# Batch 0's queries and keys loaded as whole rows of nine tokens, in a kernel of attention and two expert layers

## The chip, the cores and the metric

One core of a Trainium2 chip runs the whole program. The metric is the device time of one execution in microseconds, and less is better. The core has TensorE (PE) for products, VectorE (DVE), ScalarE (ACT) and GpSimd (POOL) for work on elements, and SyncE (SP), whose queue issues nearly all of this kernel's transfers.

## The reference

Three blocks follow each other. Attention has 4 batches, 8 heads, 576 tokens of 64 numbers, all float32. It is the sum of two parts: a pooled one, in which queries, keys and values are means over groups of four tokens, and a local one, in which a token sees only tokens less than four away. The result, 2304 rows of 512, goes through a layer with ELU (512 to 2048 to 512) and a gated layer with SiLU (512 to 1536 to 512). The weights are given in double precision.

```python
q_d = q.reshape(B, H, Sd, 4, D).mean(axis=3)           # k_d, v_d alike
out_up = np.repeat(sm_attn(q_d, k_d, v_d), 4, axis=2)  # softmax attention, scaled
scores = np.where(np.abs(pos[:, None] - pos[None, :]) < 4, scale * q @ k.T, -1e9)
x = out_up + softmax(scores) @ v                       # as rows of (batch, token)
h = x @ w_in
x = np.where(h > 0, h, np.exp(np.minimum(h, 0)) - 1) @ w_out
return (silu(x @ w_gate) * (x @ w_val)) @ w_o2
```

## The kernel before

The order in which each engine works is fixed when the program is built. A planner (class `Work`) holds a list of tasks; `add` gives each one its engine or engines, an assumed cost, a due time and the tasks and buffers that it needs. `run` plays them through on assumed clocks and lets each engine take the ready task with the earliest key; the instructions are written in the order so found, and every engine runs its own in that order, waiting on semaphores. `urge` replaces the due times of everything that the first product of the first layer needs by the length of the chain that still follows. The constants in capitals (`SECOND`, `START`, `STEP`, `LATE`, ...) are due times, offsets and penalties of the planner. They change no computation, only the order.

The first layer takes 288 rows of x (a chunk, three units of 96 tokens) at a time through 16 steps, one for each 128 columns of `w_in`: a product with a piece of `w_in` (L1010 to L1012, three products each, with both sides split in a high and a low part), the ELU on ScalarE and VectorE, and a product with `w_out`. Chunk 0's second product (L1044) uses plain float32. Each piece of weights comes as 512 KB in double precision and is made into words by ScalarE (L515, L509) and VectorE (L513, L519, through a PSUM bank) and split by a cast (L352, L356) and a subtraction on GpSimd (L554).

Chunk 0 can begin when its three units of batch 0 are through attention, so what stands ahead of it is a start-up, and there the change lies:

- `load_ident`, `load_mask`, `warm_up` and `clear` (L1692 to L1720): the identity, the masks, seven products that feed TensorE nothing of use, and a clear of the transposed queries `qT` and keys `kT`, whose margins must be zero.
- `add_first_batch` (L719): for each pair of heads p, half u of the tokens, and queries or keys, a load of 72 rows (L728; a row has four tokens of each of two heads, 1 KB a head), eight products with the identity that turn it (L734), a copy out of PSUM to `qT` or `kT` (L352 on ScalarE, L354 on VectorE), and a sum over each four tokens (`add_sums`: L620 on VectorE, or L625 and L626 on GpSimd).
- `add_pooled` (L785), for each pair of heads of batch 0: two loads of values (L800), sums of them on GpSimd (L795, L796), the score products (L812), maxima (L819, L820), exps (L825), norms (L831 to L835), transposes of the weights (L850) and the products with the values (L866).
- `add_local` (L630), for each unit: its values' loads (L595), score products (L640), mask, maximum, exps, sum, weights (L658 to L680), a spread into a block matrix (L352), products with the values (L709).
- `add_split` (L979): the two parts of attention are added (L987), and x is split for the first layer in a cast and a subtraction (L998).

The later batches come by other ways (`add_turned`, `add_pooled_all`), while the first layer's products run. The second layer follows at the end.

Of the kernel before, what the change touches and what calls it, by code (L numbers as in the profile page):

```python
# [9 lines left out]
F32 = mybir.dt.float32  # L10
# [9 lines left out]
P = 128  # L20
R = 4
# [5 lines left out]
U = NB * SB  # L27
CR = 64
NEG = -1e9
UPC = 3  # L30
# [106 lines left out]
class Work:  # L137
# [4 lines left out]
    LATENCY = 0.15  # L142
    SECOND = 43.48
    CHANGE = 0.15
# [157 lines left out]
def attention_moe_moe(ctx: ExitStack, tc: tile.TileContext, q, k, v, w_in, w_out, w_gate, w_val, w_o2, ident_in, mask_in, band_in, picks_in, out):  # L302
    nc = tc.nc
    B, H, S, D = q.shape
    FF1 = w_out.shape[0]
    FF2 = w_o2.shape[0]
    G = S // R
# [67 lines left out]
    def att_bank(late=False):  # L375
        return banks.new(lambda: [4, 5] if late or begun else [6, 0, 1, 2, 3, 7])
# [5 lines left out]

    STEP2 = 7.68
    START = 42.2
    STEP0 = 4.8
    STEP = 4.66
    FIRST = -40.0
    VALUES = -84.37
    LATER = 168.39
    POOLED = -4.59  # L390
    EARLY = -2.13
    PREFER = -27.09
    EAGER = 40.21
    URGENT = 26.74
    FREE = 7.77
    SLACK = 0.0
    LOAD = 14.4
    KEEP0 = 4.31
    KEEP1 = 1.69
    DIRECT = 2, 3, 1  # L400
    PARTS1 = 57.15
    UNIT1 = 2.61
    LAGG = 2
    MASK = -16.54
    TAILW = True
    WOS0 = 30.76
    WOS1 = 0.93
    EARLYA = 22.91
    EARLYB = 12.5
    LOADA = 53.93  # L410
    LOADB = -5.71
    O2A = 62.58
    O2B = 29.71
    ELU1 = 19.39
    ELU0 = 19.41
    UNIT2 = 22.59
    UNIT0 = 10.8
    RAW = 31.93
    DEPTH = 6
    PARTS = 13.09  # L420
    OUT = -5.4
    SUMS = 8.14
    SUMS3 = 11.07
    SECOND2 = 14.25
    LATE = 82.24
    AWAY0 = 1.99
    AWAY1 = 6.63
    LO1 = 15.73
    HI1 = 11.94
    LO2 = 26.21  # L430
    HI2 = 28.33
    LO3 = 26.82
    HI3 = 0.91
    KEYS = 34.63
    POOL1 = -7.86
    POOL0 = 10.55
    POOL2 = 13.16
    LOCAL = 0.63
    ROWS = 24.96
    INPUT = -2.86  # L440
    order = [(c, f) for c in range(NC) for f in range(NF1)]
# [106 lines left out]
    def add_weight_split(key, due, w, copiers=COPIER, second=0):  # L548
# [25 lines left out]

    PAD, LONG = R - 1, S + 8
    turned = {
        name: pools["att"].tile(shape, F32, tag=name, name=name)
# [141 lines left out]
    def add_first_batch(rows, ready):  # L719

        sums[0] = sum_ring.new()
        parts = {name: [longs[name].new(lambda p=p: [p]) for p in range(NP)] for name in ("qT", "kT")}
        made = {}
        for k, (p, u, which) in enumerate((p, u, which) for p in range(NP) for u in range(2) for which in range(2)):
            name, start = (("qT", 0), ("kT", PAD))[which]
            t, dst, pt = rows[k], parts[name][p], att_bank()
            cols = slice(start + u * UPC * U, start + (u + 1) * UPC * U)
            add("sp", 0.5, FIRST + 0.5 * k, lambda t=t, p=p, u=u, name=name: nc.sync.dma_start(  # L728
                out=t.t, in_=rows_of(name[0], 0, u, 2 * p, 2 * p + 2)), writes=[t], nbytes=HALF * 2048 * 1.2)

            def turn(t=t, pt=pt):
                for r in range(R):
                    for j in range(2):
                        nc.tensor.matmul(  # L734
                            pt.t[j * D:(j + 1) * D, :UPC * U].rearrange("c (g r) -> c g r", r=R)[:, :, r],
                            t.t[:, j, r * D:(r + 1) * D], ident[:HALF, :HALF], start=True, stop=True)

            add("pe", 0.56, FIRST + k - EAGER, turn, reads=[t], writes=[pt, dst], slack=SLACK, kind="small", after=ready[:1], words=32)
            made[which, p, u] = add(COPIER, (0.41, 0.45), FIRST + k + 1, lambda engine, dst=dst, pt=pt, cols=cols: copy(
                engine, dst.t[:, cols], pt.t[:, :UPC * U]), reads=[pt], writes=[dst], second=1)  # L740
            summed.setdefault((0, p), []).append(add_sums(
                FIRST + k + 2, lambda dst=dst, cols=cols: dst.t[:, cols].rearrange("p (g r) -> p g r", r=R),
                lambda which=which, p=p, u=u: sums[0].t[:, which, p, u * HALF:(u + 1) * HALF], [], [sums[0]], (0.45, 0.73),
                holds=[dst], after=[made[which, p, u]], engines=EITHER))
        return parts, made
# [38 lines left out]

    def add_pooled(b, p, due, load_due, raws, pr, prT):  # L785

# [11 lines left out]
        for u in range(2):  # L798
            t = raws[u]
            add("sp", 0.5, load_due, lambda u=u, t=t: nc.sync.dma_start(  # L800
                out=t.t, in_=rows_of("v", b, u, 2 * p, 2 * p + 2)), writes=[t], nbytes=HALF * 2048 * 1.2)
            rowed.append(add("pool", 1.18, due, lambda t=t: add_rows(t.t), reads=[t]))


# [58 lines left out]
        def values():  # L863
            for j in range(2):
                for w in range(2):
                    nc.tensor.matmul(  # L866
                        pv.t[j * D:(j + 1) * D, :G], raws[w].t[:, j, :D], prT.t[:, j, w], start=(w == 0), stop=(w == 1))

        valued.append(add("pe", 1.4, due + 6 - EAGER, values, words=16, reads=[prT], holds=raws, after=rowed, writes=[pv, xdT[b]], slack=SLACK, kind="small"))
        add(COPIER, (0.28, 0.3), due + 6.5 - FREE, lambda engine: copy(engine, xdT[b].t[:, p], pv.t[:, :G]), reads=[pv], writes=[xdT[b]], second=1)  # L870
# [789 lines left out]
    with tc.manual_schedule():  # L1660
# [8 lines left out]

        rows = [x for _ in range(2 * NP) for x in parts(2)]  # L1670
        vals = [x for _ in range(NU // 2) for x in parts(2)]
        praws = [x for _ in range(NP) for x in parts(2)]
# [3 lines left out]
        sms = [Part(x.whole, x.whole.t.rearrange("p a b -> p (a b)")[:, 4 * G:4 * G + H * QB].bitcast(F32).rearrange("p (n h k) -> p n h k", n=1, h=H))  # L1676
               for x in (*probs, rows[0], rows[4])]
        turneds = [Part(rows[4 * p].whole, probs[p].t) for p in range(NP)]
        for t in turneds:
            t.t = t.whole.t.rearrange("p a b -> p (a b)")[:HALF, :4 * G].bitcast(F32).rearrange("p (j u k) -> p j u k", j=2, u=2)  # L1680
        for t in rows + praws:
            t.t = t.t[:HALF].rearrange("p (h x) -> p h x", h=2)

# [19 lines left out]
        add("pe", 1.5 + 0.42 * WARM, -1000.0, warm_up)  # L1703
        add("pool", 4.8, -1000.0, clear)
        add("act", 2.0, -1000.0, table)
# [20 lines left out]
        for n in range(NU):  # L1726
            late = n >= UPC
            add("sp", 2.0, LATER + n if late else VALUES + n, lambda n=n: load_values(0, n * U, vals[n].t), writes=[vals[n]], nbytes=P * H * D * 4 * 3.1)
            turned_by = [t for (which, p, u), t in made.items() if u == (late or 0) or (which and (n == UPC - 1 or n == UPC))]
            if n == UPC:  # L1730
                for p in range(NP):
                    add_pooled(0, p, POOLED + 1.7 * p, -28 + p, raws=praws[2 * p:2 * p + 2], pr=probs[p], prT=turneds[p])
            xfs[n], = add_local(n, 1, 0.1 * n + LATE * late, parts, turned_by, [vals[n]], ready[1:], valued if late else (), sms[n])
# [92 lines left out]
```

## Time and profile before

| | |
|---|---|
| median of 3 runs | 938.55 us (938.22 to 938.77) |
| the profiled execution | 937.54 us, its span 935.8 us |
| TensorE busy | 913.0 us (98%) |
| VectorE, ScalarE, GpSimd busy | 566.3, 523.1, 533.6 us |
| mean granted TensorE clock | 0.978 of 2.4 GHz |

The span runs from the first to the last instruction of the profiled execution. The granted clock is what the throttle lets TensorE have: 1.00 is 2.4 GHz, 0.50 is 1.2 GHz. A float32 product appears in the records as two matmuls and two weight loads, a transpose as one. `SPq` is SP's queue, `PEld` TensorE's weight loads.

### The profile page before, as it was taken

Reading aid. Unit: us, or ns where it says so; the run is one execution under the profiler, and the core shown is the slowest. Engines: PE = TensorE matmul, PEld = TensorE weight load, DVE = VectorE, ACT = ScalarE, POOL = GpSimd, SP = SyncE. Lnnn points to the kernel's source line nnn. Section 1 sums busy time; section 2 is a strip of 40 time slices with the busy share of each in tenths; the row PEclk is TensorE's granted clock in tenths of the full one; section 3 lists DMA queues with packets and bytes.
Section 4 is the critical chain, followed back from the end, with each engine's and each line's share of the span. In section 5 each row is a group of like instructions: output and inputs, shape, how many; then the busy total and the mean of one; then the engine's idle time right before and its main releaser. Section 6 shows DMA issues by size and latency. Waiting matters only on the chain.

```text
span 935.8 us, 19972 instructions
## 1 busy us (share of the span) xinstructions
PE 913.0 (98%) x7573; PEld 829.0 (89%) x7573; DVE 566.3 (61%) x937; ACT 523.1 (56%) x1125; POOL 533.6 (57%) x609
## 2 busy tenths in 40 slices
PE   8779999999999999999999999999999999999998
PEld 7568889999999999999999888887888887999998
DVE  2988777777677249444337385435434247896773
ACT  3988566454556457675665456555546435453441
POOL 6797956664665459489791408998899940000000
PEclk7589999999999999999999999999999999999999
DMA  6999445659745654565588613452554299854331
GB/s 172 309 270 276 82 125 126 139 178 315 132 114 152 189 186 140 163 204 195 187 296 326 247 61 124 169 191 91 210 181 183 104 350 308 273 170 135 127 113 46
DMA packets 194704, 172.12 MB, mean 184 GB/s; under 512 B 96176, under 2 KB 166192, under 8 KB 194608
## 3 DMA queue, kind: packets, MB, share of 16 engines
q1 hardware_dynamic: 194464, 170.58, 58.2%
q8 instruction: 60, 0.98, 0.4%
q14 instruction: 36, 0.29, 0.1%
q10 hardware_dynamic: 144, 0.26, 0.1%
HBM read 111.62 MB, written 59.18 MB: 183 GB/s over the span
## 4 chain that ended last, share of the span: by engine, by line
PE 91%; DMA 4%; DVE 2%; SPq 1%; ACT 1%; issue 1%; POOL 0%; DVEq 0%
PE bank L1010 28%; PE bank L1011 27%; PE bank L1012 27%; PE bank L1044 3%; PE bank L640 2%; PE bank L709 2%; DMA w<-in_v_dram 2%; DMA w<-in_moe_w_in_dram 1%; DMA w<-in_k_dram 1%; PE bank L915 1%; PE bank L909 1%; PE bank L962 1%; DVE xh L1191 1%; SPq L595 0%; DMA wd<-mid 0%
## 5 line engine op out<-in xcount | busy, mean ns | idle before, releaser
L1010 PE MATMUL bank<-xs,wu 128*128 128x512 f32 x336 | 133.4, 397 | 2.4 <-DVE blk L1223 2.0
L1012 PE MATMUL bank<-xs,wu 128*128 128x512 f32 x336 | 133.2, 396 | 0.0
L1011 PE MATMUL bank<-xs,wu 128*128 128x512 f32 x336 | 133.2, 396 | 0.0
L1010 PE MATMUL bank<-os,ys 128*128 128x256 f32 x378 | 107.2, 283 | 1.0 <-DVE o L1223 1.0
L1011 PE MATMUL bank<-os,ys 128*128 128x256 f32 x378 | 107.0, 283 | 0.0
L1012 PE MATMUL bank<-os,ys 128*128 128x256 f32 x378 | 106.9, 283 | 0.0
L1010 PE MATMUL bank<-x,w 128*128 128x288 f32 x320 | 100.2, 313 | 1.4 <-DVE e L1088 0.9
L1010 PE MATMUL bank<-g,w 128*128 128x288 f32 (+1 forms) x320 | 101.0, 316 | 0.0
L1223 DVE TENSOR_TENSOR blk<-bank,blk 128x512 f32<-128x512 f32 x72 | 49.5, 690 | 81.7 <-PE bank L1012 75.4
L1011 PE MATMUL bank<-g,w 128*128 128x288 f32 (+1 forms) x320 | 98.5, 308 | 0.0
L1012 PE MATMUL bank<-g,w 128*128 128x288 f32 (+1 forms) x320 | 98.3, 307 | 0.0
L1011 PE MATMUL bank<-x,w 128*128 128x288 f32 x320 | 95.3, 298 | 0.0
L1012 PE MATMUL bank<-x,w 128*128 128x288 f32 x320 | 94.9, 296 | 0.0
L1095 POOL TENSOR_TENSOR g<-e,g 128x288 fp32r<-128x288 f32 x64 | 57.2, 894 | 56.0 <-ACT g L352 44.7
L1220 ACT COPY blk<-bank 128x512 f32<-128x512 f32 x72 | 42.0, 585 | 72.9 <-PE bank L1012 66.0
L1010 PEld LDWEIGHTS bank<-xs,wu 128*128 128x128 f32 x336 | 63.3, 188 | 17.7 <-DVE blk L1223 2.9
L1012 PEld LDWEIGHTS bank<-xs,wu 128*128 128x128 f32 x336 | 63.3, 188 | 15.4
L1011 PEld LDWEIGHTS bank<-xs,wu 128*128 128x128 f32 x336 | 63.3, 188 | 14.0
L1010 PEld LDWEIGHTS bank<-os,ys 128*128 128x128 f32 x378 | 72.5, 192 | 1.6 <-DVE o L1223 1.4
L1011 PEld LDWEIGHTS bank<-os,ys 128*128 128x128 f32 x378 | 72.5, 192 | 0.1
L1012 PEld LDWEIGHTS bank<-os,ys 128*128 128x128 f32 x378 | 72.5, 192 | 0.0
L1191 POOL TENSOR_TENSOR wu<-s,wu 128x256 fp32r<-128x256 f32 x79 | 59.7, 783 | 18.5 <-ACT wu L1194 18.4
(213 smaller groups left out, 2525.3 us busy)
## 6 DMA issues: line engine op xcount, KB each, us to landing
yr<-yd SPq DMA_DIRECT2D x27, 512.0 KB
yd<-blk SPq DMA_DIRECT2D x24, 512.0 KB
os<-od SPq DMA_DIRECT2D x42, 256.0 KB
w<-in_moe_w_in_dram SPq DMA_DIRECT2D x16, 512.0 KB
w<-in_moe_w_out_dram SPq DMA_DIRECT2D x16, 512.0 KB
wp<-w SPq DMA_DIRECT2D x16, 512.0 KB
wu<-wp SPq DMA_DIRECT2D x16, 512.0 KB
u<-wd SPq DMA_DIRECT2D x32, 256.0 KB
```

Of the source, the lines that this page charges most:

```text
L640: nc.tensor.matmul(sc[j].t[s * QB:(s + 1) * QB, (u * NP + p) * QB:(u * NP + p + 1) * QB], parts["qT"][p].t[j * D:(j + 1) * D, a:a + QB], p ...
L709: nc.tensor.matmul(pvs[u].t[j * D:(j + 1) * D, p * U:(p + 1) * U], tvs[u].t[:, (2 * p + j) * D:(2 * p + j + 1) * D], bd.t[:, u, j * NP + p ...
L909: nc.tensor.matmul(sc[0].t[j * D:(j + 1) * D, 2 * G:3 * G], vs0.t[:, w, j], prT0.t[:, j, w], start=(w == 0), stop=(w == 1))
L915: nc.tensor.matmul(sc[j].t[:HALF, u * G:(u + 1) * G], t[:, 0, p, u * HALF:(u + 1) * HALF], t[:, 1, p], start=True, stop=True)
L1010: nc.tensor.matmul(ps, sh, mh, start=first, stop=False, skip_group_check=more)
L1011: nc.tensor.matmul(ps, sh, ml, start=False, stop=False, skip_group_check=more)
L1012: nc.tensor.matmul(ps, sl, mh, start=False, stop=last, skip_group_check=more)
L1044: nc.tensor.matmul(acc[0][i].t[:, :T1], wo.t[:, i * P:(i + 1) * P].bitcast(F32), ge(), start=f == 0, stop=f == NF1 - 1)
L1095: add("pool", 0.86, due - URGENT, lambda e=e, g=g: nc.gpsimd.tensor_tensor(out=g.t[:, 1], in0=e.t, in1=g.t[:, 0], op=ALU.subtract), reads= ...
L1191: return task(engines, n, due, lambda engine=engines[0]: two(engine).tensor_tensor(out=out(), in0=in0(), in1=in1(), op=op), reads, writes, ...
L1220: return add("act", ps_copy, when(m) - 20, lambda: nc.scalar.copy(d(i), ps.t[:, :w]), reads=[ps], writes=of(i))
L1223: return add("dve", ps_sum, when(m) - 20, lambda: nc.vector.tensor_tensor(out=d(i), in0=ps.t[:, :w], in1=d(i), op=ALU.add), reads=[ps], wr ...
```

## The change

Batch 0's queries and keys are loaded as 128 rows (two heads times 64 groups of nine tokens), one load for each pair of heads. Each is turned by eighteen products of 64 rows, five tokens into one PSUM bank and four into another; two copies put them in place with a stride of nine. One sum over each pair of heads takes the place of two. Every local unit of batch 0 now waits for all copies. The pooled values come in one load for each pair, in rows of eight tokens, so that the pooled queries and keys are taken alternately instead of by halves. The clear touches only the margins of `qT` and `kT`. The planner's costs and its constants are set anew.

```diff
-    SECOND = 43.48
+    SECOND = 37.4
-    START = 42.2
-    STEP0 = 4.8
-    STEP = 4.66
+    START = 43.14
+    STEP0 = 4.77
+    STEP = 4.73
...
-    VALUES = -84.37
-    LATER = 168.39
+    VALUES = -89.48
+    LATER = 136.26
...
+    NINE = S // D
...
+    def rows9(name, b, h0, h1):
+        return source[name][b, h0:h1].rearrange("h (g r) d -> (h g) (r d)", r=NINE)
+    def rows8(name, b, h0, h1):
+        return source[name][b, h0:h1].rearrange("h (p r) d -> p h (r d)", r=2 * R)
...
-        for k, (p, u, which) in enumerate((p, u, which) for p in range(NP) for u in range(2) for which in range(2)):
+        for k, (p, which) in enumerate((p, which) for p in range(NP) for which in range(2)):
...
+            full = dst.room.make(p)[:, start:start + S]
+            add("sp", 0.5, FIRST + 1.0 * k, lambda t=t, p=p, name=name: nc.sync.dma_start(
+                out=t.t, in_=rows9(name[0], 0, 2 * p, 2 * p + 2)), writes=[t], nbytes=P * NINE * D * 4)
+            of = []
+            for u, (r0, n) in enumerate(((0, 5), (5, NINE - 5))):
+                pt, to = att_bank(), full.rearrange("c (g r) -> c g r", r=NINE)[:, :, r0:r0 + n]
+                def turn(t=t, pt=pt, r0=r0, n=n):
+                    for r in range(n):
+                        for j in range(2):
+                            h = slice(j * D, (j + 1) * D)
+                            nc.tensor.matmul(
+                                pt.t[h, :S // NINE * n].rearrange("c (g r) -> c g r", r=n)[:, :, r],
+                                t.t[h, (r0 + r) * D:(r0 + r + 1) * D], ident[h, h], start=True, stop=True)
+                add("pe", 0.11 * n, FIRST + 2 * k + u - EAGER, turn, reads=[t], writes=[pt, dst], slack=SLACK, kind="small", after=ready[:1], words=4 * n)
+                of.append(add(COPIER, (0.19 + 0.05 * n, 0.16 + 0.07 * n), FIRST + 2 * k + u + 1, lambda engine, to=to, pt=pt, n=n: copy(
+                    engine, to, pt.t[:, :S // NINE * n].rearrange("c (g r) -> c g r", r=n)), reads=[pt], writes=[dst], second=1))
+            made[which, p] = of
             summed.setdefault((0, p), []).append(add_sums(
-                FIRST + k + 2, lambda dst=dst, cols=cols: dst.t[:, cols].rearrange("p (g r) -> p g r", r=R),
+                FIRST + 2 * k + 3, lambda full=full: full.rearrange("p (g r) -> p g r", r=R),
...
-        def add_rows(t):
+        def add_rows():
+            t = raw.t.rearrange("p h (w x) -> p (h w) x", w=2)
             half = t[:, :, :2 * D]
...
-            rowed.append(add("pool", 1.18, due, lambda t=t: add_rows(t.t), reads=[t]))
+        add("sp", 0.5, load_due, lambda: nc.sync.dma_start(
+            out=raw.t, in_=rows8("v", b, 2 * p, 2 * p + 2)), writes=[raw], nbytes=HALF * 4096 * 1.15)
+        rowed.append(add("pool", 2.05, due, add_rows, reads=[raw]))
...
-                        sc[j].t[:HALF, u * G:(u + 1) * G], t[:, 0, p, u * HALF:(u + 1) * HALF], t[:, 1, p], start=True, stop=True)
+                        sc[j].t[:HALF, u * G:(u + 1) * G], t[:, 0, p].rearrange("c (g u) -> c g u", u=2)[:, :, u], t[:, 1, p], start=True, stop=True)
...
-                            pws[j].t[:HALF, w * G + u * HALF:w * G + (u + 1) * HALF],
-                            pr.t[:, j, u, w * HALF:(w + 1) * HALF], ident[:HALF, :HALF])
+                            pws[j].t[:HALF, w * G:(w + 1) * G].rearrange("k (g u) -> k g u", u=2)[:, :, u],
+                            pr.t[:, j, u].rearrange("q (k w) -> q k w", w=2)[:, :, w], ident[:HALF, :HALF])
...
         def clear():
-            for name in ("qT", "kT"):
-                nc.gpsimd.memset(turned[name], 0.0)
+            q, k = (turned[name].rearrange("p (n l) -> p n l", n=NP) for name in ("qT", "kT"))
+            nc.gpsimd.memset(q[:, :, S:], 0.0)
+            nc.gpsimd.memset(k[:, :, :PAD], 0.0)
+            nc.gpsimd.memset(k[:, :, PAD + S:], 0.0)
...
-            turned_by = [t for (which, p, u), t in made.items() if u == (late or 0) or (which and (n == UPC - 1 or n == UPC))]
+            turned_by = [t for ts in made.values() for t in ts]
```

Some 65 further constants of the planner are changed in the same way.

## Rows read from the trace of the kernel before

**Rows 1.** The page's busy times: us, share of the span, instructions, by engine.

```profile
PE 913.0 (98%) x7573; PEld 829.0 (89%) x7573; DVE 566.3 (61%) x937; ACT 523.1 (56%) x1125; POOL 533.6 (57%) x609
```

**Rows 2.** Stretches: us; PE, PEld, DVE, ACT, POOL busy; clock, DMA share, GB/s.

```profile
10.00:12.50 2.50, 2.50 (x47) 2.50 (x45) 0.00 (x0) 0.84 (x3) 0.00 (x0) 0.50 0.85 204
...
30.00:40.00 10.00, 7.41 (x62) 6.39 (x64) 9.20 (x27) 9.52 (x29) 7.54 (x9) 0.50 1.04 379
...
0.00:19.50 19.50, 17.75 (x299) 14.99 (x299) 3.12 (x7) 7.73 (x18) 10.85 (x25) 0.71 0.67 181
19.50:52.50 33.00, 20.95 (x384) 17.55 (x367) 30.36 (x74) 26.48 (x79) 25.58 (x36) 0.60 0.92 264
...
52.50:935.80 883.30, 874.28 (x6923) 796.47 (x6910) 532.77 (x857) 488.91 (x1030) 497.13 (x550) 1.00 0.57 181
```

**Rows 3.** The chain of waits in the start-up: start us, us, what.

```profile
25.59 0.46 SPq L469
...
52.63 0.54 PE bank L1010
```

**Rows 4.** Timeline, 0 to 20 us: start, us, instruction, [idle before, releaser].

```profile
1.19 0.44 SPq L728 DMA_DIRECT2D w<-in_q_dram  x1
...
2.72 2.04 POOL L1696 MEMSET kT<- 128x2336 f32 x1
...
4.29 1.40 PE L734 MATMUL bank<-ident,w 72*64 72x72 f32 x32
...
6.15 0.57 PEld L734 LDWEIGHTS bank<-ident,w 72*64 72x64 f32 x16 [0.61 <-DMA w<-in_q_dram]
...
15.40 0.40 ACT L352 COPY kT<-bank 128x288 f32<-128x288 f32 x1 [0.56 <-PE bank L734]
...
19.13 0.89 PE L640 MATMUL bank<-kT,qT 64*32 64x32 f32 x64
```

**Rows 5.** Short stretches, L734 alone: us; PE, PEld busy; clock, DMA share, GB/s.

```profile
7.40:7.80 0.40, 0.40 (x12) 0.28 (x10) 1.00 0.79 205
...
8.20:8.60 0.40, 0.40 (x11) 0.40 (x9) 0.50 0.83 223
```

**Rows 6.** Timeline just ahead of the first layer's first product.

```profile
51.16 0.31 PE L640 MATMUL bank<-kT,qT 64*32 64x32 f32 x2 [5.60 <-DVE w L519]
...
52.03 0.99 POOL L998 TENSOR_TENSOR x<-f,x 128x384 fp32r<-128x384 f32 x1
```

**Rows 7.** The page's DMA issues; a row for keys reads the same.

```profile
w<-in_q_dram SPq DMA_DIRECT2D x8, 144.0 KB
```

**Rows 8.** Groups by line and shape, 0 to 52.6 us: busy us, mean ns.

```profile
L519 DVE SCALAR_TENSOR_TENSOR w<-bank,w 128x512 int32<-128x512 int32 x9 | 5.9, 678 | 0.3 <-ACT bank L509 0.3
...
L554 POOL TENSOR_TENSOR w<-w 128x512 fp32r<-128x512 f32 x4 | 5.1, 1274 | 3.5 <-ACT w L352 3.4
...
L812 PEld LDWEIGHTS bank<-sums 64*72 64x72 f32 x32 | 3.5, 207 | 2.8 <-DVE w L658 1.8 <-POOL w L796 0.5 <-ACT w L825 0.4
...
L352 ACT COPY qT<-bank 128x288 f32<-128x288 f32 x8 | 3.2, 399 | 6.6 <-PE bank L734 6.6
...
L620 DVE TENSOR_REDUCE sums<-kT 128x72 f32<-128x288 f32 x6 | 2.7, 445 | 6.2 <-ACT kT L352 6.2
```

**Rows 9.** VectorE's timeline, 16 to 23 us.

```profile
20.10 0.49 DVE L658 TENSOR_TENSOR w<-bank,mask 128x128 f32<-128x128 f32 x2 [3.46 <-POOL w L796]
20.51 0.44 DVE L620 TENSOR_REDUCE sums<-kT 128x72 f32<-128x288 f32 x1
...
22.31 0.81 DVE L819 TENSOR_REDUCE mx<-bank 72x2 f32<-72x288 f32 x2
```

**Rows 10.** GpSimd's timeline, 13 to 29 us.

```profile
13.06 0.42 POOL L625 TENSOR_TENSOR half<-qT 128x144 f32<-128x144 f32 x1 [5.59 <-ACT qT L352]
...
16.93 0.72 POOL L795 TENSOR_TENSOR w<-w 72x256 f32<-72x256 f32 x1
...
28.25 0.45 POOL L796 TENSOR_TENSOR w<-w 72x128 f32<-72x128 f32 x1
```

More of the change, by code (lines that the diff above doesn't have):

```diff
@@ L379, in bank @@
         return banks.new(lambda: places)
-    STEP2 = 7.68
-    START = 42.2
-    STEP0 = 4.8
-    STEP = 4.66
+    STEP2 = 7.66
+    START = 43.14
+    STEP0 = 4.77
+    STEP = 4.73
     FIRST = -40.0
-    VALUES = -84.37
-    LATER = 168.39
[L390 to L395, printed above, removed]
+    VALUES = -89.48
+    LATER = 136.26
+    POOLED = -3.76
+    EARLY = -0.32
+    PREFER = -29.07
+    EAGER = 48.84
+    URGENT = 20.38
+    FREE = 7.43
     SLACK = 0.0
-    LOAD = 14.4
-    KEEP0 = 4.31
-    KEEP1 = 1.69
+    LOAD = 13.42
+    KEEP0 = 3.75
+    KEEP1 = 1.45
     DIRECT = 2, 3, 1
-    PARTS1 = 57.15
-    UNIT1 = 2.61
+    PARTS1 = 84.06
+    UNIT1 = 2.84
     LAGG = 2
-    MASK = -16.54
+    MASK = -15.51
     TAILW = True
[L406 to L418, printed above, removed]
-    DEPTH = 6
[L420 to L440, printed above, removed]
+    WOS0 = 38.79
+    WOS1 = -1.52
+    EARLYA = 33.6
+    EARLYB = 13.05
+    LOADA = 69.71
+    LOADB = 2.47
+    O2A = 17.15
+    O2B = 30.37
+    ELU1 = 37.28
+    ELU0 = 19.82
+    UNIT2 = 24.89
+    UNIT0 = 12.26
+    RAW = 20.73
+    DEPTH = 6
+    PARTS = 25.22
+    OUT = -5.83
+    SUMS = 6.09
+    SUMS3 = 17.3
+    SECOND2 = 15.91
+    LATE = 77.51
+    AWAY0 = 2.14
+    AWAY1 = 6.55
+    LO1 = 13.69
+    HI1 = 16.38
+    LO2 = 24.04
+    HI2 = 25.84
+    LO3 = 27.24
+    HI3 = -1.16
+    KEYS = 47.43
+    POOL1 = -7.89
+    POOL0 = 13.45
+    POOL2 = 16.61
+    LOCAL = 2.09
+    ROWS = 18.68
+    INPUT = -7.3
     order = [(c, f) for c in range(NC) for f in range(NF1)]
@@ L723, in add_first_batch @@
         made = {}
-        for k, (p, u, which) in enumerate((p, u, which) for p in range(NP) for u in range(2) for which in range(2)):
+        for k, (p, which) in enumerate((p, which) for p in range(NP) for which in range(2)):
             name, start = (("qT", 0), ("kT", PAD))[which]
[L726 to L740, printed above, removed]
@@ new lines, in add_first_batch @@
+            t, dst = rows[k], parts[name][p]
+            full = dst.room.make(p)[:, start:start + S]
[14 more added lines that the diff above has]
+                    engine, to, pt.t[:, :S // NINE * n].rearrange("c (g r) -> c g r", r=n)), reads=[pt], writes=[dst], second=1))
@@ L741, in add_first_batch @@
+            made[which, p] = of
             summed.setdefault((0, p), []).append(add_sums(
-                FIRST + k + 2, lambda dst=dst, cols=cols: dst.t[:, cols].rearrange("p (g r) -> p g r", r=R),
-                lambda which=which, p=p, u=u: sums[0].t[:, which, p, u * HALF:(u + 1) * HALF], [], [sums[0]], (0.45, 0.73),
-                holds=[dst], after=[made[which, p, u]], engines=EITHER))
+                FIRST + 2 * k + 3, lambda full=full: full.rearrange("p (g r) -> p g r", r=R),
+                lambda which=which, p=p: sums[0].t[:, which, p], [], [sums[0]], (0.75, 1.13),
+                holds=[dst], after=of, engines=EITHER))
@@ L866, in values @@
                     nc.tensor.matmul(
-                        pv.t[j * D:(j + 1) * D, :G], raws[w].t[:, j, :D], prT.t[:, j, w], start=(w == 0), stop=(w == 1))
-        valued.append(add("pe", 1.4, due + 6 - EAGER, values, words=16, reads=[prT], holds=raws, after=rowed, writes=[pv, xdT[b]], slack=SLACK, kind="small"))
+                        pv.t[j * D:(j + 1) * D, :G], raw.t[:, j, w * R * D:w * R * D + D], prT.t[:, j, w], start=(w == 0), stop=(w == 1))
+        valued.append(add("pe", 1.4, due + 6 - EAGER, values, words=16, reads=[prT], holds=[raw], after=rowed, writes=[pv, xdT[b]], slack=SLACK, kind="small"))
         add(COPIER, (0.28, 0.3), due + 6.5 - FREE, lambda engine: copy(engine, xdT[b].t[:, p], pv.t[:, :G]), reads=[pv], writes=[xdT[b]], second=1)
@@ L1668, in parts @@
             return [Part(buf, buf.t[:, a].bitcast(F32)) for a in range(n)]
-        rows = [x for _ in range(2 * NP) for x in parts(2)]
+        rows = [x for _ in range(2 * NP) for x in parts(1)]
         vals = [x for _ in range(NU // 2) for x in parts(2)]
-        praws = [x for _ in range(NP) for x in parts(2)]
+        praws = [x for _ in range(NP) for x in parts(1)]
         probs = [x for _ in range(NP) for x in parts(1)]
@@ L1676, in attention_moe_moe @@
         sms = [Part(x.whole, x.whole.t.rearrange("p a b -> p (a b)")[:, 4 * G:4 * G + H * QB].bitcast(F32).rearrange("p (n h k) -> p n h k", n=1, h=H))
-               for x in (*probs, rows[0], rows[4])]
-        turneds = [Part(rows[4 * p].whole, probs[p].t) for p in range(NP)]
+               for x in (*probs, rows[0], rows[2])]
+        turneds = [Part(rows[2 * p].whole, probs[p].t) for p in range(NP)]
         for t in turneds:
             t.t = t.whole.t.rearrange("p a b -> p (a b)")[:HALF, :4 * G].bitcast(F32).rearrange("p (j u k) -> p j u k", j=2, u=2)
-        for t in rows + praws:
-            t.t = t.t[:HALF].rearrange("p (h x) -> p h x", h=2)
+        for t in praws:
+            t.t = t.whole.t[:HALF].bitcast(F32)
+        for t in rows:
+            t.t = t.whole.t.rearrange("p a b -> p (a b)")[:, :NINE * D].bitcast(F32)
         warm, zeros = pools["ps"].tile([P, 512], F32, tag="bank7", name="warm"), turned["bd"].rearrange("p n a b -> p (n a b)").bitcast(BF16)[:, :512]
@@ L1703, in attention_moe_moe @@
         add("pe", 1.5 + 0.42 * WARM, -1000.0, warm_up)
-        add("pool", 4.8, -1000.0, clear)
+        add("pool", 0.6, -1000.0, clear)
         add("act", 2.0, -1000.0, table)
```

8 lines of the change are left out of this document (2 added, 6 removed).

## Prediction

> **What bounds the kernel now.** I read the page's busy shares first. TensorE is busy for 913.0 us, 98% of the span [rows 1], so only what lets it begin sooner, or gives it less to do, can shorten the kernel. The table of stretches shows where its idle time lies: from 52.5 us to the end at 935.8 it is busy for 874.28 of 883.30 us, at full clock; the 52.5 us before that are the start-up [rows 2]. The chain of waits puts the first product of the first layer at 52.63 us [rows 3], and from there on the matmuls follow each other. The change touches only the start-up's code, besides the planner's constants. So the question is by how much 52.6 us moves.
>
> The same table tells what kind of stretch the start-up is. In the first 19.5 us VectorE works for 3.12 us, in the 33 us behind it for 30.36, with ScalarE at 26.48 and GpSimd at 25.58 [rows 2]. The first part is paced by transfers and turns, the second by the three vector engines. The timeline gives the border: the first score products (L640) start at 19.13 us, right behind the last turn (L734) [rows 4].
>
> Inside the first part there are two paces. Until about 8 us the granted clock is 1.00 (2.4 GHz), from 8.2 us it is 0.50 (1.2 GHz), although TensorE is busy with turns for all of both slices [rows 5]: turns have taken the place of the dense warm-up products. At the low clock each copy that follows a turn takes 0.40 us and stands idle for 0.56 before it, until its turn is done [rows 4]: one turn, 8 products of 72 columns, takes 0.96 us, 120 ns a product. At full clock the weight loads of the turn at 6.15 took 0.57 us for the eight, 71 ns a product [rows 4].
>
> At the other end of the start-up two chains meet. One is of weights: the L640 in front of the first product stood for 5.60 us until VectorE's L519, which frees a PSUM bank, and ran just ahead of 52.63 [rows 3, 6]. The other is that of x: GpSimd's last L998 starts at 52.03 and ends at 53.02 [rows 6], and the first layer multiplies what it writes. Both have to move for the kernel to gain.
>
> **The change, part by part.** *Transfers.* Queries and keys were 16 loads of 144 KB, 2.36 MB [rows 7]; they become 8 of 288 KB, each row 2,304 B long where it was two pieces of 1,024. From 10 to 12.5 us the transfers ran at 204 GB/s and a share of 0.85; from 30 to 40, with the longer weight rows, at 379 and 1.04 [rows 2]. 2.36 MB take 11.6 us at the first rate and 6.2 at the second. A row of 2,304 B over 128 partitions is nearer to the weight loads, so I take 6.2, with 11.6 as the other bound. Eight q/k issues of about 0.4 us and four of the pooled values also go from SP's queue [rows 4]; the value issues and the weight loads behind them, which begin at 25.59 us [rows 3], come some 5 us sooner. That is relief for the weight chain, not for x.
>
> The Trainium skill, "DMA: Bandwidth & Descriptors", section "Why a DMA increments its semaphore by 16 and not by 1", says that a DMA is spread over the largest number of engines up to 16 that divides the slowest dimension of both sides: 12 for 72 rows, 16 for 128. The share of 0.85 against 1.04 [rows 2] agrees with that roughly. By the rule alone, at unchanged speed of an engine, the q/k time falls to three quarters, 8.7 us as an estimate from the row's 11.6. The pooled values keep 72 rows and would stay at 12.
>
> *Turns.* Before: 16 turns of 8 products, 128 products of 72 rows by 72 columns. After: 8 tiles, each of nine tokens times two heads = 18 products, 144 of 64 by 64. No row shows a 64-by-64 product. Before, the two heads of a turn already ran in different halves of the output; after, they use different halves of the rows too. I scale with the columns: 120 x 64/72 = 107 ns at the low clock and 71 x 64/72 = 63 ns at the high one, so 1.92 or 1.14 us a tile. At the low clock the whole is 144 x 107 = 15.4 us, and before it was 128 x 120 = 15.4: the products themselves give nothing back. What does is the spell at full clock, in which before the rows came too slowly. The first load was issued at 1.19 and its products began at 4.29 [rows 4]; a load of twice the size costs 0.2 us more, so I start at 4.5. If the clock falls at 8.2 as now, 3.7/1.14 = 3.25 tiles are done by then; the other 4.75 take 9.1 us, and the turns end at 17.3 and not at 19.13. **-1.8 us.** Bounds: all at the low clock 4.5 + 15.4 = 19.9 (+0.8), all at the high one 4.5 + 9.1 = 13.6 (-5.5). At 379 GB/s a tile lands each 0.8 us and is not waited for; at 204 it would be each 1.4, so 2.6 tiles by 8.2 and 1.2 us lost again.
>
> *Copies.* Sixteen of 288 columns at 399 ns [rows 8] become eight of 320 and eight of 256, with the same sum of columns, written in runs of five or four. Zero: ScalarE idles for 0.56 us before each at the low clock [rows 4]. If short runs cost more than that, only the last copy shows it: between 0 and half of 0.4 us.
>
> *Sums.* Sixteen sums of 288 columns, 0.445 us each on VectorE [rows 8], become eight of 576, at most 0.89 each. What matters is where they stand. VectorE idled for 3.46 us until 20.10, then three old sums, the first at 20.51, ran in front of the first pooled maxima at 22.31 [rows 9], from which the exps follow. That is 1.33 us on x's path. With whole tiles in order, all but the last tile's sum can be done while turns run; that one costs 0.89 or goes to GpSimd. Bounds -1.3 and -0.4; I take **-0.9 us.**
>
> *Pooled values.* GpSimd's eight pairs of row sums (0.72 + 0.45 us on 256 and 128 elements [rows 10], 9.4 us in all) become four pairs on 512 and 256; at (0.72 - 0.45)/128 = 2.1 ns an element that is 1.26 + 0.72 = 1.98 each, 7.9 us. They ran from 16.93 to 28.70 between other steps of x's path [rows 10]. Their rows come sooner, into time when GpSimd idled (5.59 us before 13.06 [rows 10]). Between 0 and -1.5, **-0.3 us**, since VectorE, not GpSimd, is the fuller engine here.
>
> *The rest.* GpSimd's second clear of 2.04 us, from 2.72 [rows 4], and the first like it shrink to the margins. They are hidden: they end at 4.76, while the first turn is still running; uncovered, they would hold up the first copy alone. Pooled scores, transposes and values keep their counts; stationaries or outputs now step over every second element. No row has that for a stationary; the turns' outputs stepped by four at the pace of their columns, so I take zero. If each of the 32 stationaries of L812, 3.5 us in all [rows 8], took twice as long, it would be 3.5 us more, against 12 idle us of TensorE between 19.5 and 52.5 [rows 2], so at most some 1 us on the path.
>
> *The constants.* They redraw the order of everything in the first layer. After 52.5 us there are 9.0 idle us to win or to add to [rows 2]. I put this at zero and keep it for the range.
>
> Sum: -1.8 - 0.9 - 0.3 = -3.0 us. The profiled execution took 937.54 us, 1.74 beyond its span of 935.8, and would become 934.5. It lies 1.01 below the median of the runs, 938.55, which would become 935.55, so **935.5**.
>
> **The rivals.** *The clock holds through the turns (16 in 100).* Without a wait for rows TensorE may keep its 2.4 GHz. Against it: it fell at 8.2 us in the midst of turns [rows 5]. The turns would end at 13.6, 3.7 sooner than forecast: about 932.
>
> *The weight side holds the start (20 in 100): no measurable change.* The 5.60 us of L640 for L519 [rows 6] are hidden only since x came at 53.02. If x comes at 50 and the redrawn order leaves weight words in front as late as now, the start stays at 52.6: about 938. For it: the vector engines are filled to nine tenths by words and x together [rows 2]. Against it: the weight transfers move up by some 5 us.
>
> *The same place, slower (14 in 100).* The new order puts one weight more in front of the first product. Its L519 and its GpSimd split L554 cost 0.678 + 1.274 = 1.95 us [rows 8]. It decides as soon as the words that free the bank end later than 53.0. Then the gain of x is lost and up to 1.95 us come on top: 940.5.
>
> *The redrawn order also removes waits behind 52.5 us (6 in 100)*: half of the 9 idle us, about 931.
>
> **How the numbers follow.** The forecast has 44 in 100, with its own range 934 to 937.2: the sums and rows between their bounds, and the turns at the pace of either transfer rate. A change of 0.2%, 1.9 us, is about what a measurement of this kernel tells from none. Faster: forecast, clock and order, 44 + 16 + 6 = 66 in 100. Same: 20. Slower: 14. The range goes from 931.2 (leaving out the last rival's better half and the far bound of the clock) to 939.3 (leaving out most of the slower one).
>
> **What the profile will show.** Eight L728 of 128 rows each, at over 300 GB/s between 3 and 10 us; the last L734 product near 17, with pairs of copies 1.9 us apart at the low clock; VectorE's first pooled maxima near 19.5; weight loads from about 20; the first L1010 near 49.6; behind it TensorE without new gaps. The prediction is wrong if the 64-row products run at another pace than their columns say, if the clock falls elsewhere, or if the first layer's first product waits for weight words rather than for x.

## The result and the profile after

The changed kernel takes 945.62 us (943.91 to 946.27, 4 runs) against 938.38 us for the kernel before; the ratio is 1.0076, 95% interval 1.0058 to 1.0093. It is slower by some 7 us, where 935.5 was forecast. The profiled execution took 945.59 us with a span of 943.3. In the new file the names of the code have other lines: loads of q and k L737, turns L747, local scores L649, pooled rows L810 and L811, pooled scores L824, maxima L831, the first layer's products L1022 to L1024; in the second layer, which uses the same products, L1235 (VectorE) adds a product to what is there, L1232 (ScalarE) copies one, L1271 makes weight words, and L1203 combines two tiles by a difference, a sum or a product.

The page's busy row of after, as [rows 1]:

```profile
PE 911.0 (97%) x7605; PEld 825.5 (88%) x7605; DVE 572.6 (61%) x937; ACT 520.5 (55%) x1119; POOL 529.4 (56%) x598
```

TensorE works 2 us less than before and the span is 7.5 longer: TensorE stands still more. The table of stretches of after (columns as in [rows 2]) says where:

```profile
5.00:10.00 5.00, 5.00 (x153) 4.94 (x153) 0.00 (x0) 3.27 (x8) 2.29 (x5) 1.00 0.96 336
...
0.00:19.50 19.50, 14.11 (x347) 11.38 (x348) 6.06 (x11) 10.02 (x26) 9.60 (x23) 1.00 0.75 207
19.50:50.40 30.90, 21.40 (x476) 17.91 (x475) 27.65 (x70) 24.14 (x68) 20.77 (x24) 0.61 0.88 268
50.40:943.30 892.90, 875.54 (x6796) 796.17 (x6783) 538.89 (x857) 486.35 (x1025) 499.06 (x553) 1.00 0.57 179
```

The transfers do what the change wants (336 GB/s) and the clock stays at 1.00 through the turns, where it fell at 8.2 us before [rows 5]. But in the first 19.5 us TensorE now idles for 5.4 us against 1.75, and behind the first product of the first layer for 17.4 against 9.0 [rows 2]. TensorE's timeline of after shows the first of these:

```profile
4.29 7.41 PE L747 MATMUL bank<-ident,w 64*64 64x64 f32 x213
13.27 2.43 PE L747 MATMUL bank<-ident,w 64*64 64x64 f32 x75 [1.57 <-issue]
15.63 0.72 PE L824 MATMUL bank<-sums 64*72 64x144 f32 x8
16.28 0.59 PE L649 MATMUL bank<-kT,qT 64*32 64x32 f32 x44
19.72 0.43 PE L649 MATMUL bank<-kT,qT 64*32 64x32 f32 x20 [2.85 <-issue]
...
50.50 0.61 PE L1022 MATMUL bank<-x,w 128*128 128x288 f32 x1
...
57.81 0.40 PE L1022 MATMUL bank<-x,w 128*128 128x288 f32 x1 [2.08 <-DVE g L1063]
```

The same row of before:

```profile
58.17 0.40 PE L1010 MATMUL bank<-x,w 128*128 128x288 f32 x1 [0.51 <-DVE g L1051]
```

The last turn ends at 15.70, 3.4 us ahead of the 19.13 at which the local scores of before followed its last turn [rows 4]. Twice TensorE stands though no other engine keeps it ("issue"), for 4.42 us together: once within the turns and once within the local scores, each time in the middle of equal products. The first product of the first layer comes at 50.50 and not at 52.63 [rows 3]; the product that waits for the first step's ELU comes at 57.81, where before has 58.17. So 2.1 us of lead are 0.4 a step later.

Of the 8.3 us by which the idle time behind the first product grew, 3.5 lie from 150 to 350 us, after and then before:

```profile
150.00:350.00 200.00, 196.11 (x2441) 185.19 (x2429) 121.12 (x243) 100.54 (x243) 111.85 (x142) 1.00 0.62 166
```

```profile
150.00:350.00 200.00, 199.61 (x2534) 189.67 (x2534) 128.76 (x250) 106.85 (x255) 113.57 (x143) 1.00 0.63 171
```

Most of it, 2.6 us, is again stops for "issue". The other half of the growth lies far behind. What TensorE waited for from 600 to 800 us, after and then before (us in total, times, the longest):

```profile
PE bank L1022 <- DVE blk L1235: 5.1, 3, 2.0
PE bank L1022 <- ACT blk L1232: 0.9, 1, 0.9
PE bank L1022 <- DVE blk L1569: 0.4, 1, 0.4
```

```profile
PE bank L1010 <- DVE blk L1223: 2.0, 2, 1.2
PE bank L1010 <- ACT blk L1220: 0.4, 1, 0.4
```

Here TensorE waits until the second layer's products are taken out of their PSUM banks into `blk`. Of the code of this layer the diff has no line, only constants.

### The profile page after: what moved, and what is told of

It reads as the page before. It is cut to its first block, busy times and chain, and to the rows that moved or that the text cites. A ratio compares the mean times of both kernels' runs of the same rounds, so it can differ in the third digit from the quotient of the medians.

```text
span 943.3 us, 19985 instructions
## 1 busy us (share of the span) xinstructions
PE 911.0 (97%) x7605; PEld 825.5 (88%) x7605; DVE 572.6 (61%) x937; ACT 520.5 (55%) x1119; POOL 529.4 (56%) x598
## 5 line engine op out<-in xcount | busy, mean ns | idle before, releaser
L1022 PE MATMUL bank<-xs,wu 128*128 128x512 f32 x336 | 134.4, 400 | 6.1 <-DVE blk L1235 5.1
L1024 PE MATMUL bank<-xs,wu 128*128 128x512 f32 x336 | 133.9, 398 | 0.0
L1022 PE MATMUL bank<-os,ys 128*128 128x256 f32 x378 | 107.1, 283 | 0.5 <-DVE o L1235 0.5
L1024 PE MATMUL bank<-os,ys 128*128 128x256 f32 x378 | 107.1, 283 | 0.0
L1022 PE MATMUL bank<-x,w 128*128 128x288 f32 x320 | 100.4, 314 | 2.8 <-DVE g L1063 2.1
L1022 PE MATMUL bank<-g,w 128*128 128x288 f32 (+1 forms) x320 | 101.1, 316 | 0.0
L1024 PE MATMUL bank<-g,w 128*128 128x288 f32 (+1 forms) x320 | 98.4, 308 | 0.0
L1235 DVE TENSOR_TENSOR blk<-bank,blk 128x512 f32<-128x512 f32 x72 | 49.5, 689 | 79.5 <-PE bank L1024 72.9
L1024 PE MATMUL bank<-x,w 128*128 128x288 f32 x320 | 94.7, 296 | 0.0
L1232 ACT COPY blk<-bank 128x512 f32<-128x512 f32 x72 | 42.0, 584 | 76.6 <-PE bank L1024 71.5
L1022 PEld LDWEIGHTS bank<-xs,wu 128*128 128x128 f32 x336 | 63.7, 190 | 22.5 <-DVE blk L1235 6.7
L1024 PEld LDWEIGHTS bank<-xs,wu 128*128 128x128 f32 x336 | 63.5, 189 | 15.5
L1022 PEld LDWEIGHTS bank<-os,ys 128*128 128x128 f32 x378 | 72.5, 192 | 0.9 <-DVE o L1235 0.7
L1024 PEld LDWEIGHTS bank<-os,ys 128*128 128x128 f32 x378 | 72.5, 192 | 0.1
L1203 POOL TENSOR_TENSOR wu<-s,wu 128x256 fp32r<-128x256 f32 x79 | 60.8, 796 | 14.8 <-ACT wu L1206 14.7
```

The source lines that it names most:

```text
L1022: nc.tensor.matmul(ps, sh, mh, start=first, stop=False, skip_group_check=more)
L1024: nc.tensor.matmul(ps, sl, mh, start=False, stop=last, skip_group_check=more)
L1203: return task(engines, n, due, lambda engine=engines[0]: two(engine).tensor_tensor(out=out(), in0=in0(), in1=in1(), op=op), reads, writes, ...
L1232: return add("act", ps_copy, when(m) - 20, lambda: nc.scalar.copy(d(i), ps.t[:, :w]), reads=[ps], writes=of(i))
L1235: return add("dve", ps_sum, when(m) - 20, lambda: nc.vector.tensor_tensor(out=d(i), in0=ps.t[:, :w], in1=d(i), op=ALU.add), reads=[ps], wr ...
```

## Experiments

Each was timed beside the kernel before on the same chip; the ratio is to that.

**Constants and code apart.** First the new code with the constants before, then the old code with the new constants.

```diff
-    SECOND = 37.4
+    SECOND = 43.48
...
-    INPUT = -7.3
+    INPUT = -2.86
```

> The changed code with every planner constant of the kernel before. Theory A, the loss lies in the order that the new constants draw behind the start-up (TensorE idles 8 us more behind 150 us than before) while the new loads and turns themselves pay about 2 us: 935 to 939 us. Rival B, the new loads, turns and pooled steps lose the time themselves: 943 us or more.

940.61 us, ratio 1.0018 (0.9999 to 1.0037), between the ranges of the two theories.

> The code before with every planner constant of the change. Theory A: it is slower than before, 942 to 949 us, with waits of TensorE behind 150 us. Rival B: within 0.3% of before, 936 to 941 us.

954.09 us, ratio 1.0173 (1.0142 to 1.0204), more than theory A allowed. The constants alone cost 16 us with the old code and 5 with the new.

**The planner's count of instructions.** The planner reckons with TensorE's supply of instructions by a number for each task (`words`); the new turns give 4 n for 2 n products of four instructions each.

```diff
-                add("pe", 0.11 * n, ..., kind="small", after=ready[:1], words=4 * n)
+                add("pe", 0.11 * n, ..., kind="small", after=ready[:1], words=8 * n)
```

> The changed kernel with the planner told 8 instructions for each pair of products of a turn in place of 4, nothing else; the profile shows four for each product. Theory C, the order is bad because the planner thinks that TensorE's instructions arrive sooner than they do (TensorE stood 1.57 and 2.85 us in the start-up with nothing but its own issue to wait for): 940 to 943 us, with those two waits shorter. Theory A alone: 944 to 948 us, as the changed kernel, whatever the two waits do.

954.86 us, ratio 1.0174 (1.0144 to 1.0204), above both theories.

> The changed code with the constants of before and the count of 8. Theory A with C: the lowest of the four, 933 to 937 us. A without C: as with the constants alone, 935 to 939. Rival B: 943 us or more.

944.35 us, ratio 1.0066 (1.0045 to 1.0088), in rival B's range. Counting rightly redraws the order, and both new orders are longer than the ones that they replace, so neither time speaks for the new code by itself; the next run separates the two. The stops do not settle it either: in the start they came to 4.42 us in the first of these, as in after, and to 0.93 in the second, but they differ as much between executions of one order (last section). That the wrong count makes the bad order is not borne out.

**The order held.** The program was built from the new code, but each task's place in the order, its engine and its buffer were taken from a record of the kernel before.

```diff
-        work.run()
+        work.replay()
```

> The changed kernel's loads, turns, copies, sums and pooled rows, but with the order, the engine and the bank of every task held to those of the kernel before (each new task stands where the tasks that it replaces stood), so the planner's constants have no say. Theory A (the new start-up by itself pays or is neutral, and what is lost is lost in the order that the planner draws behind it): 935 to 938 us, and behind 60 us TensorE stands idle where it did in the kernel before, about 8.5 us in all. Rival B (the new products lose time by themselves, because TensorE stands for its instructions between the turns and the first local scores): 939 to 942 us, with two waits of 1.5 to 3 us that no other engine ends in the first 20 us and the first feed-forward product no earlier than 52.5 us.

937.64 us, ratio 0.9994 (0.9972 to 1.0017), in theory A's range. Its timeline:

```profile
9.81 5.46 PE L1028 MATMUL bank<-ident,w 64*64 64x64 f32 x180 [0.25 <-DMA w<-in_q_dram]
15.21 0.82 PE L930 MATMUL bank<-kT,qT 64*32 64x32 f32 x52
16.33 0.28 PE L930 MATMUL bank<-kT,qT 64*32 64x32 f32 x12 [0.30 <-issue]
...
49.35 0.61 PE L1303 MATMUL bank<-x,w 128*128 128x288 f32 x1
```

With the old order behind it the new start has its lead: the first product at 49.35, 3.3 us sooner than in the profiled execution of before, and the waits from 600 us on are those of before to the tenth (2.0, 1.0, 0.4). What the median shows of it is 1 us, within the uncertainty; this execution lost 1.6 us again to one stop for "issue" that ended at 210 us.

**Fewer instructions.** Half of the turns as transposes, two instructions in place of four.

```diff
-                            nc.tensor.matmul(
-                                pt.t[h, ...][:, :, r], t.t[h, ...], ident[h, h], start=True, stop=True)
+                            if j == 0:
+                                nc.tensor.transpose(pt.t[h, ...][:, :, r], t.t[h, ...], ident[h, h])
+                            else:
+                                nc.tensor.matmul(
+                                    pt.t[h, ...][:, :, r], t.t[h, ...], ident[h, h], start=True, stop=True)
```

> The changed kernel with the turns of the first head of each pair written as transposes, two TensorE instructions each in place of four (72 turns: 144 instructions fewer of the 576 that the turns and their first scores stand behind). If the two waits of 1.57 and 2.85 us in the first 20 us are for instructions, they shrink to under 2.5 us together and the local scores of the first unit end 1 to 2.5 us sooner than 20.15 us; the order behind is that of the changed kernel, so the end is 942.5 to 946 us. If the waits are for something else, they stay above 4 us together.

977.25 us, ratio 1.0406 (1.0376 to 1.0436).

> Both edits: the order of the kernel before held, and half of the turns as transposes. Theory A with instruction supply as the price of the start: 933.5 to 936.5 us, 1 to 2 us under the kernel with the order held alone. Rival B': the first feed-forward product is set by the gate, scores and weights behind the start and not by the turns, and the time is that of the kernel with the order held alone within 0.5 us.

970.74 us, ratio 1.0316 (1.0280 to 1.0352). Neither theory had this. From the timeline of the first:

```profile
9.66 0.31 PE L748 MATMUL bank<-ident,w 64*64 64x64 f32 x1
9.90 0.47 PE L752 MATMUL bank<-ident,w 64*64 64x64 f32 x2
10.30 0.31 PE L748 MATMUL bank<-ident,w 64*64 64x64 f32 x1
```

A transpose (L748) and a product (L752) by turns take 0.64 us a pair, at a granted clock of 0.50, and 0.43 ahead of 8.6 us, at 1.00; two products took 0.12 to 0.14 at 1.00 in the kernels above, and 0.24 at the low clock of before. The turns last until 48.8 us, so the runs say nothing about the supply of instructions.

**The orders joined.** After again as a measure, then its start with the rest of before's order, and the other way about.

> The changed kernel once more, as the measure for the two next ones on the same chip: 944 to 947 us.

944.35 us, ratio 1.0067 (1.0051 to 1.0084). Its profiled execution was the fastest of the six, 939.85 us: TensorE idled for 2.2 us from 150 to 350 us and for 4.4 from 600 to 800, where the profile of after has 3.9 and 6.5. By as much do profiles of one order differ.

> The changed kernel's code with two recorded orders joined: the changed kernel's own order up to a feed-forward product behind the last local scores of batch 1 (1,371 of the 3,502 tasks), and the order of the kernel before behind it. Where a weight slot that the old order names is still in use, the free slot that was released first is taken. Theory A1 (most of the loss is drawn behind the attention, in the second feed-forward layer, where TensorE stood 6.5 us against 2.4 us): 938 to 941.5 us. Rival A2 (the loss is made in the start and while the attention of batch 1 runs, by the waits for instructions and the 2.5 us of stops from 200 to 300 us): 943 to 946 us.

962.70 us, ratio 1.0259 (1.0240 to 1.0279).

> The same join the other way about: the order of the kernel before (with the new tasks where the replaced ones stood) up to that product, 1,381 tasks, and the changed kernel's order behind it. Theory A1: 941.5 to 946 us. Rival A2: 936 to 940 us. If both joins come out in between, the loss is shared.

950.31 us, ratio 1.0123 (1.0094 to 1.0151). Both lie above both parents: the seam costs waits that neither parent has (one of 3.5 us for "blk" in the first, 3.4 in the second). Neither theory had this, and their times decide nothing.

**The two parts of the change, each with the order held.**

> With the order of the kernel before held: only the queries' and keys' part of the change (loads of 128 rows, products of 64 rows, copies, sums), the pooled values as before. Theory: this part makes the whole lead that the kernel with the order held had in its start. First feed-forward product at 49.2 to 50.0 us, time 935 to 938 us, within 1 us of the kernel with the whole change and the order held. Rival: the lead needs the pooled values too, and the first product comes later than 51 us.

936.92 us, ratio 0.9980 (0.9968 to 0.9992): faster than both kernels. The first product of its profiled execution, one of 940.28 us, came at 50.95, between theory and rival, and a stop for "issue" behind 150 us took 2.4 us.

> With the order of the kernel before held: only the pooled values in rows of eight, queries and keys as before. Theory: nothing waits for these rows; first feed-forward product at 52.2 to 52.9 us, time within 1 us of the kernel before (937 to 939 us). Rival: the interleaved columns of the pooled scores and transposes cost by themselves, and the time is over 939.5 us.

939.47 us, ratio 1.0004 (0.9991 to 1.0016). In the times queries and keys make the gain, the pooled rows nothing that can be measured. Its first product came at 54.14, later than expected, though its turns ended only 0.7 us later than before's; where the rest went is open. A lead read from one execution is thus uncertain by a microsecond or more.

**The constants in two groups.** The planner draws a whole order each time. First the eighteen constants that only reach the second layer go back to their old values, then all the others.

```diff
-    WOS0 = 38.79
+    WOS0 = 30.76
...
-    O2A = 17.15
+    O2A = 62.58
...
-    SECOND2 = 15.91
+    SECOND2 = 14.25
```

> The changed kernel with only the 18 constants of the second layer set back to the values before; the order is the changed kernel's up to the 1,695th task, and differs behind it. Theory A1 (the loss lies in the second layer, where TensorE waited 6.6 us for VectorE and ScalarE against 3.4): 940 to 942 us, with waits for blk of under 4 us. Rival A2 (the loss lies in the start and the first layer): 944 to 947 us. Rival A3 (any redrawing of an order that had been chosen among many costs time, whichever constants do it): over 947 us.

939.95 us, ratio 1.0011 (0.9991 to 1.0031), as theory A1 had it.

> The changed kernel with all other constants (start and first layer) set back and the 18 of the second layer kept new. Theory A1: 944 to 947 us, waits for blk of 5 to 7 us. Rival A2: 939 to 942 us. Rival A3: over 947 us.

946.03 us, ratio 1.0080 (1.0051 to 1.0108), again as A1 had it. With both groups old it was 1.0018, with both new 1.0076 and 1.0067: the second layer's constants cost some 0.6%, 5 to 6 us, the others nothing that can be measured. The waits point the same way. From 560 us on, with the second layer's constants old, then with the others old (whose profiled execution, 953.02 us, was the slowest of its seven, so that no time is read from it):

```profile
PE bank L1022 <- DVE blk L1235: 2.0, 2, 1.2
PE bank L1022 <- DVE o L1235: 1.0, 2, 0.5
PE bank L1022 <- ACT blk L1232: 0.4, 1, 0.4
```

```profile
PE bank L1022 <- DVE blk L1235: 5.2, 3, 2.0
PE bank L1022 <- ACT blk L1232: 0.9, 1, 0.9
PE bank L1022 <- DVE o L1235: 0.5, 1, 0.5
PE bank L1022 <- DVE blk L1569: 0.4, 1, 0.4
```

What makes these waits stands in the timelines of the engines of after, here VectorE's single instructions of over 4 us from 600 to 800:

```profile
616.66 4.74 DVE L1271 SCALAR_TENSOR_TENSOR u<-u,r 128x512 int32<-128x512 int32 x1
...
645.37 4.26 DVE L1271 SCALAR_TENSOR_TENSOR u<-u,r 128x512 int32<-128x512 int32 x1
...
685.44 4.54 DVE L1271 SCALAR_TENSOR_TENSOR u<-u,r 128x512 int32<-128x512 int32 x1
...
738.27 6.02 DVE L1203 TENSOR_TENSOR blk<-blk 128x512 f32<-128x512 f32 x1
```

GpSimd at the same time:

```profile
613.59 7.27 POOL L1203 TENSOR_TENSOR blk<-blk 128x1024 f32<-128x1024 f32 x4
...
646.68 2.40 POOL L1203 TENSOR_TENSOR blk<-blk 128x1024 f32<-128x1024 f32 x1
...
682.71 6.03 POOL L1203 TENSOR_TENSOR blk<-blk,sg 128x1024 f32<-128x1024 f32 x3
688.70 0.73 POOL L1203 TENSOR_TENSOR s<-u 128x256 f32<-128x256 f32 x1
...
742.31 1.43 POOL L1203 TENSOR_TENSOR wu<-u,wu 128x256 fp32r<-128x256 f32 x2
```

and TensorE:

```profile
623.26 0.51 PE L1022 MATMUL bank<-xs,wu 128*128 128x512 f32 x1 [1.67 <-DVE blk L1235]
...
650.28 0.50 PE L1022 MATMUL bank<-xs,wu 128*128 128x512 f32 x1 [1.42 <-DVE blk L1235]
...
692.59 0.50 PE L1022 MATMUL bank<-xs,wu 128*128 128x512 f32 x1 [0.90 <-ACT blk L1232]
...
745.54 0.50 PE L1022 MATMUL bank<-xs,wu 128*128 128x512 f32 x1 [2.01 <-DVE blk L1235]
```

Of the thirteen L1271 from 600 to 800 us seven take under 1.0 us, the shortest 0.67. The four long instructions have one thing in common: each ends some 0.55 us behind the end of a run of GpSimd instructions without a pause (620.86, 649.08, 689.43 and 743.74), so it lasted through three to eight of them. What is queued behind it on VectorE, the sum into `blk`, is late; the third holds up ScalarE too, and with it the copy (L1232) that TensorE waits for:

```profile
690.01 0.63 ACT L1560 ACTIVATE sg<-blk 128x512 f32<-128x512 f32 x1 [2.75 <-DVE u L1271]
```

Within 0.7 to 2.6 us of each such end TensorE goes on again after a stand, of 6.0 us in the four places. The kernel before has one instruction of over 4 us in this stretch, the kernel with the second layer's old constants one, that with the others old four. The second profile of after's own order (the changed kernel again) has the first three, but the fourth came through:

```profile
736.33 1.18 DVE L1203 TENSOR_TENSOR blk<-blk 128x512 f32<-128x512 f32 x1
```

There the wait of 2.0 us behind it is gone too, in the same instructions in the same order.

## Why the prediction was wrong

The step that failed is *the constants*, "I put this at zero". They are worth some +0.6%, 5 to 6 us, and those of the second layer make it. I had argued about "the order of everything in the first layer" and about 9 idle us behind the start; the constants of the start and the first layer cost nothing that can be measured, and the waits were added 600 us behind the place that I looked at. The zero had no row behind it. That the loss comes by VectorE's long instructions beside GpSimd is read from rows, the two profiles of one order above all; no run moved only them. In these rows the waits from 600 to 800 us grew by 4.0 us in one profile and by 2.0 in the other, so that 1 us or more of the 5 to 6 is in no row.

The Trainium skill, "SBUF — State Buffer", section "Who interferes with whom", says that a VectorE instruction with two SBUF inputs contends with a GpSimd instruction that reads SBUF. The long instructions agree; that one can stand through a whole run of GpSimd instructions, as the 6.02 us through eight of them, is what these rows add.

*Turns, -1.8:* right in sign, too small. The condition of the rival "the clock holds" (16 in 100) came true, its time of 932 did not: the granted clock stayed at 1.00 and with the order held the turns ended at 15.27, 3.9 us sooner; 180 matmuls in 5.46 us are 61 ns a product, against 63 forecast. The 0.2 us for a load of twice the size had no row behind it; the first product began at 4.29 as before. And no step had TensorE stop for "issue", which took back 4.42 us in after.

*Transfers:* 336 GB/s against 379 assumed; with the order held two waits for a tile of q came to 1.1 us. The Trainium skill, "DMA: Bandwidth & Descriptors", section "Why a DMA increments its semaphore by 16 and not by 1", let 72 rows use 12 engines and 128 rows 16. The share of 0.96 beside 0.85 [rows 2] goes that way; the rate rose by more than the rule's third, from 204 to 336, and the longer rows changed with it; no run parts the two.

*Copies, 0:* 463 ns for 320 columns and 412 for 256, in sum 0.6 us more than before [rows 8], hidden. *Sums, -0.9:* 0.75 us for a whole tile; in after the first pooled maxima ran at 16.58 and not at 22.31 [rows 9], but the second at 21.34 only, behind the stop. With the order held the first ran at 19.24, 3.1 us sooner, less than the turns' 3.9: the sums gave nothing beyond the turns. *Pooled rows, -0.3:* 1.27 + 0.73 = 2.0 us a pair as forecast, and no time.

*Sum to the first product, -3.0:* with the order held -3.3 in its one profile. That the two agree is luck: the turns alone gave 3.9 where 1.8 was forecast, and sums and pooled rows, -1.2 together, gave nothing. How much of it lasts to the end was not forecast right: -1.0 by the medians and -0.6 by the ratio (-2.6 to +1.6 by the interval) with the whole change, -1.9 (-3.0 to -0.8) with queries and keys alone. "Behind it no new gaps" was wrong: besides the second layer's waits, the new turns bring stops for "issue" behind the start (last section). The rival of the weight side ("vector engines filled to nine tenths" holds for VectorE alone; ScalarE has 80% and GpSimd 78% of [rows 2]) did not decide either: with the order held the scores in front of the first product still stood for weight words, for 5.62 us, but 3.2 us sooner. And a weight more in front of the first product did not happen: that product came sooner.

Between the old constants with a free order (1.0018) and the held order (0.9994) lie 2 us, not clear of noise, that the planner's redrawn start and first layer may take; which wait makes them is open.

## What to carry to other kernels

When constants of a planner change with the code, build the new code under the old order first, and time the constants by themselves: here the code was worth 0 to -2 us and the constants +5 to +6, in a layer that the code doesn't touch. Read the whole trace for what a redrawn order can do, not only the part around the edit. A lead in the start counts only if the next step is ready for it.

## What was not expected of the hardware

**Stops for "issue" differ from one execution to the next.** Five profiled executions of the same order of instructions in the start stopped at the same place, with 20 of the first 64 matmuls of the local scores left, for 2.85 us (after), 3.67 (after again), 0.66 (the new code with the old constants), 0.93 and 5.59:

```profile
16.44 0.32 PE L649 MATMUL bank<-kT,qT 64*32 64x32 f32 x20 [0.93 <-issue]
```

```profile
20.86 0.43 PE L649 MATMUL bank<-kT,qT 64*32 64x32 f32 x20 [5.59 <-issue]
```

The first is the kernel with the second layer's constants old, the second that with the others old. The page counts 60 transfers of 16 KB for instructions, one for 254 of TensorE's 15,210 matmuls and weight loads, and the two stops of after's start stand just 254 of them apart (75, 8 and 44 matmuls, each with its load). The trace has the time of each such transfer: in all sixteen profiles together TensorE stopped 43 times for "issue" for over 0.25 us, and every stop ended 1.2 to 1.8 us behind the landing of one. So these stops are waits for blocks of instructions, as far as rows can show it; no run moved a block on purpose. In the start the transfer began at 13.89 us where the stop took 0.93, and at 18.20 where it took 5.59; why it began later is open. The three profiles with the old turns have no such stop of over 0.3 us. Of the thirteen with the new turns all but one lost 0.8 to 3.9 us to them between 100 and 400 us; this is part of the lead that did not last. That it comes of the changed count of instructions in front of every later block (64 more in after) is argued, not shown. The Trainium skill, "Runtime: NRT & Kernel Launch", section "Instruction fetch mechanics", says that instructions come in blocks of 16 KiB and that the cost of crossing into one is mostly hidden; the 60 transfers agree, the stops do not: these crossings did not hide.

**Transposes by turns with products are slow:** 0.43 to 0.64 us a pair, where two products take 0.12 to 0.24. Which part of it is the change between the two, and which the transpose itself, was not tried.

**The record of the clock and the pace can part.** With the pooled rows alone, the old turns ran 256 matmuls in 15.63 us, 122 ns a product, the pace of [rows 4] at 0.50, while the granted clock of that stretch reads 1.00:

```profile
4.29 15.63 PE L1020 MATMUL bank<-ident,w 72*64 72x72 f32 x256
```

The half transposes do the same: with the order held they took 0.64 us a pair at a recorded 1.00, as without it at 0.50. Whether the record is off there or something else slowed these turns is not shown. A pace read from the matmuls themselves stands in any case.
